# Row-sum reciprocals transposed in the tails' step, weighted sums one step later, one bank for each engine

## The chip, the cores and the metric

One core of a Trainium2 chip runs the whole program. The metric is the time of one execution on the device, in microseconds; a measurement is the median of several runs. TensorE (PE) multiplies matrices into PSUM, VectorE (DVE) and ScalarE (ACT) read PSUM and compute, GpSimd (POOL) works from SBUF alone, and SyncE (SP) issues the transfers. Each engine takes its instructions in the order in which the program puts them, and waits at an instruction for the semaphores that it names.

## The reference

An attention layer with a positional bias from a small network feeds a mixture of eight experts (one for each token), and that a gated feed-forward layer:

```python
scores = scale * np.matmul(q, k.transpose(0, 1, 3, 2))      # 4 batches, 8 heads, 576 x 576, head size 64
scores = scores + bias.transpose(2, 0, 1)[None, :, :, :]
scores = scores - np.max(scores, axis=-1, keepdims=True)
attn = np.exp(scores)
attn = attn / (np.sum(attn, axis=-1, keepdims=True) + 1e-09)
attn_out = np.matmul(attn, v)
...
h = np.maximum(x[mask] @ w1[e], 0.0)
out[mask] = gate_w[mask, None] * eom[mask, e, None] * (h @ w2[e])
...
return (silu * val @ w_out)
```

The change lies in the attention: the exponentials are multiplied by v before they are divided, and the division by the row sums is done on the product.

## The kernel before

The program computes the bias tables first, then the attention, then the experts, then the feed-forward layer. The attention is a loop over 16 **units**, a pair of heads p and a batch b each, and every unit has five **steps** c = 0 to 4 (c0 to c4 below). In c0 to c3 a step takes 128 queries of both heads, in c4 the last 64 queries of both heads at once, the one head on partitions 0 to 63 and the other on 64 to 127.

One pass of the loop over (unit, step) writes down, in this order, what goes into the engines' queues, and this hand-written order is what the chip follows (`tc.manual_schedule()`):

- **S** (s_pe, L255): PE multiplies queries and keys into a tile of two banks. There are two such tiles (pool pS, bufs=2); c0 to c3 need both, c4 needs one.
- **T** (t_pe, L288, L304, L305): PE transposes the exponentials of the step before the last one (`old`) into the tile T of two banks. 64x128 pieces on partitions 0 to 63 go to bank 0, those on 64 to 127 to bank 1. At c4 the `old` step is c2, and the tails (block 4) of c0 and c1 are transposed too, into **Tx**, the second of the pS tiles. At c1 `old` is c4 of the unit before.
- ACT's share of emptying T (t_ev with act=1, L309), into the tiles pt0 and pt1.
- **pv** (pv_list, L364): the matmuls of transposed exponentials by v, for the first 256 queries (list A, tile pv0) and the other 320 (list B, tile pv1). PVA and PVB say how many of a list's five go into which step.
- **s_max** (L259, DVE) adds the bias and finds the row's limit; **exp** (L264, ACT) makes the exponentials and the row sums.
- DVE's share of emptying T and Tx (t_ev with act=0, L311).
- **rps** (bc_recip, L347, L349, L352), in c1 and c3: the reciprocals of the sums, spread out along rows in the tiles rw and rt by POOL (p_recip), are transposed by PE into the free one of the pv banks and copied by ACT into the tile rb.
- p_recip (c0): DVE adds 1e-9 and takes reciprocals; POOL writes rw (L338) and rt (L340).
- **e0** (in c2 of the next unit) and **e1** (in c0 of the unit after that): DVE multiplies a finished pv tile by rb into xT (L370).
- one of the four pieces of the next unit's preparation on POOL: k_hi, k_lo, q_hi, q_lo (prep_qk).

DVE and ACT share T by columns: DVE takes the pieces 0 to 3 of both banks, ACT 4 to 7. In the last two units the router of the first batch runs in the loop's gaps (moe_early, at the places LG); behind the loop the last two `old` steps, the rest of the pv list (pvq) and the first expert steps (h_step, y_step) are written one by one.

Of the kernel before, what the change touches and what calls it, by code (L numbers as in the profile page):

```python
# [30 lines left out]
PVA = {4: 1, 5: 2, 6: 2}  # L31
PVB = {7: 2, 8: 2, 9: 1}
BL = (20, 28, 30, 32, 36)
VL = (7, 12, 13, 14)
LG = (1, 5, 5, 7, 8, 10, 10)
# [74 lines left out]
def body(tc, qt, kt, va, vb, ws, moe_w_gate, moe_w_output_gate, moe_w1, moe_w2, w_gate, w_val, w_out, ctab, cst, cst2, out):  # L110
    nc = tc.nc
    with ExitStack() as ctx:
# [27 lines left out]
        blocks, ident2 = const.tile([128, 128], F32, name="blocks"), const.tile([128, 64], F32, name="ident2")  # L140
# [149 lines left out]
        def t_pe(c, Es, x):  # L290

            t, E = tb["t"], Es[-1]
            if c == 2:
                for i in range(2):
                    t_blk(Es[i], x, 64 * i, 4)
            if c < 4:
                for j, n in enumerate((0, 1, 2, 3, 5, 6, 7, 8)):
                    t_blk(E, t, 64 * j, n)
            else:
# [4 lines left out]
                nc.tensor.transpose(t[0:64, 0, 384:448], E[0:64, 512:576], ident[0:64, 0:64])  # L304
                nc.tensor.matmul(t[64:128, 0, 384:448], E[64:128, 0:64], ident[64:128, 64:128], start=True, stop=True)  # L305
# [7 lines left out]
        def t_ev(p, b, c, x, act):  # L313

            t, pt = tb["t"], pts[p, b]
            if c < 4:
                o, n = 128 * (c % 2), 4 * act
                copy(act, pt[c // 2][:, n:n + 4, o:o + 128].rearrange("p n (r t) -> p r n t", r=2),
                     t[:, :, 64 * n:64 * n + 256].rearrange("p r (n t) -> p r n t", n=4))
                if c == 2 and not act:  # L320
                    copy(0, pt[0][:, 8].rearrange("p (c r t) -> p r c t", c=2, r=2), x[:, :, 0:128].rearrange("p r (c t) -> p r c t", c=2))
            elif act:
                copy(1, pt[1][:, 8, 0:256].rearrange("p (c r t) -> p r c t", c=2, r=2), t[:, :, 256:384].rearrange("p r (c t) -> p r c t", c=2))
                copy(1, pt[1][:, 8, 256:320], t[:, 0, 384:448])
# [6 lines left out]
        def p_recip(st):  # L331
# [3 lines left out]
            def f():  # L335
# [3 lines left out]
                rbs["t"] = ap.tile([128, S], F32, tag="E", bufs=4, name="rt")[:, 0:128]  # L339
                nc.gpsimd.tensor_scalar(rbs["t"], blocks, st[:, 38:39], None, ALU.mult)  # L340
            late.append(f)

        def bc_recip(p, b, st, f):

            ps, w = pv_tile(1 - f, "rps"), (256, 320)[f]
            for c in range(2):
                nc.tensor.transpose(ps[:, 128 * c:128 * c + 128], rbs["w"][:, 256 * f + 128 * c:256 * f + 128 * c + 128], ident)  # L347
            if f:
                nc.tensor.matmul(ps[:, 256:320], rbs["t"], ident2, start=True, stop=True)  # L349
            else:  # L350
# [436 lines left out]
        def consts():  # L787
            nc.gpsimd.memset(blocks, 0.0)
            for r in range(2):
                k = slice(64 * r, 64 * r + 64)  # L790
                nc.gpsimd.memset(blocks[k, k], 1.0)
# [531 lines left out]
```

## Time and profile before

| what | us |
|---|---|
| median of 3 runs | 1038.69 (1036.95 to 1039.5) |
| the profiled execution | 1042.37 |
| its span on the core | 1040.5 |
| PE busy | 995.6 (96%) |
| DVE busy | 574.5 (55%) |
| ACT busy | 439.7 (42%) |
| POOL busy | 123.9 (12%) |

The profile is of one execution. Busy shares are means over the whole program; the attention stage (about 85 to 320 us) has a balance of its own, which the stretches show. In a timeline an engine's instructions of one form that follow each other stand in one row: start, time, engine, line, operation, output and input tiles, count, and in brackets how long the engine was idle before it and what ended that. The end of a matmul is modelled, so that rows overlap by some tenths; the start of the next row tells better how long PE was with one. A float32 matmul that isn't a transpose makes two records.

### The profile page before, as it was taken

To read this page: it belongs to the slowest core of one execution; us is meant where nothing else is said; L and a number is where in the kernel's file an instruction comes from. 1 tells how busy PE (TensorE), PEld (TensorE's weight loads), DVE (VectorE), ACT (ScalarE), POOL (GpSimd) and SP (SyncE) were. 2 spreads that over 40 slices of the span, in tenths; PEclk is the share of its full clock that TensorE was granted. 3 is DMA by queue.
4 is the path that set the end of the run, shared out by engine and by line. 5 is a ranking of instruction groups with operands and counts; after the bars stand their busy time and mean duration, and the time that the engine had idled before them with its cause. 6 is when DMAs were issued, how large, how long until landed. Compare 5 with 4: busy or idle time off the path is not lost. (4 is left out here: it accounts for less than half of the span.)

```text
span 1040.5 us, 18771 instructions
## 1 busy us (share of the span) xinstructions
PE 995.6 (96%) x7477; PEld 802.3 (77%) x7477; DVE 574.5 (55%) x1257; ACT 439.7 (42%) x931; POOL 123.9 (12%) x122
## 2 busy tenths in 40 slices
PE   7978999999999999999999899999999999999998
PEld 2346767677667899998999677778888888888897
DVE  8966777677776654445565599952223223222322
ACT  6766766676665442332434445531113112211221
POOL 3662442433220000000000000000000000000000
PEclk9988999999999999999999999999999999999999
DMA  6774223342004052814733655511002000200010
GB/s 189 209 250 140 94 93 109 109 126 96 24 22 155 1 198 68 293 64 143 253 108 142 211 172 172 166 53 48 1 0 82 1 1 1 61 1 1 18 24 21
DMA packets 67754, 101.89 MB, mean 98 GB/s; under 512 B 9136, under 2 KB 37936, under 8 KB 67664
## 3 DMA queue, kind: packets, MB, share of 16 engines
q1 hardware_dynamic: 67504, 100.41, 30.5%
q8 instruction: 59, 0.97, 0.4%
q14 instruction: 31, 0.25, 0.1%
q10 hardware_dynamic: 160, 0.26, 0.1%
HBM read 74.63 MB, written 26.03 MB: 97 GB/s over the span
## 5 line engine op out<-in xcount | busy, mean ns | idle before, releaser
L1218 PE MATMUL v<-x,w 128*128 128x512 f32 (+1 forms) x720 | 161.5, 372 | 3.8 <-DVE w L967 3.8
L1218 PE MATMUL g<-x,w 128*128 128x512 f32 (+1 forms) x720 | 159.8, 371 | 2.1 <-DVE xl L722 2.0
L1218 PEld LDWEIGHTS v<-x,w 128*128 128x128 f32 x720 | 125.4, 189 | 32.1 <-DVE w L967 7.5
L1218 PEld LDWEIGHTS g<-x,w 128*128 128x128 f32 x720 | 127.4, 189 | 27.0 <-ACT x L1173 2.2
L1240 PE MATMUL o<-w,uh 128*128 128x512 f32 x432 | 133.4, 390 | 0.0
L1221 DVE TENSOR_TENSOR t<-g,t 128x512 f32<-128x512 f32 (+1 forms) x60 | 38.2, 636 | 169.6 <-ACT t L1220 169.6
L259 DVE CUSTOM_DVE_ANT_0 E<-S,bias 128x576 f32<-128x576 f32 x128 | 91.9, 755 | 47.4 <-PE S L255 24.3
L264 ACT ACTIVATE E<-E,st 128x576 f32<-128x576 f32 x144 | 110.0, 768 | 4.7 <-DVE st L259 4.7
L1220 ACT ACTIVATE t<-g 128x512 f32<-128x512 f32 (+1 forms) x60 | 33.2, 554 | 155.2 <-PE g L1218 155.2
L1225 ACT ACTIVATE uh<-t 128x512 fp32r<-128x512 f32 (+1 forms) x60 | 35.4, 589 | 146.0 <-DVE t L1222 146.0
L364 PE MATMUL pv<-pt,rawv 128*64 128x256 f32 (+1 forms) x640 | 95.5, 419 | 0.0
L255 PE MATMUL S<-kh,qz 64*128 64x288 f32 (+1 forms) x576 | 85.3, 328 | 10.5 <-DVE pt L311 6.4
L1240 PEld LDWEIGHTS o<-w,uh 128*128 128x128 f32 x432 | 80.3, 188 | 16.1
L255 PEld LDWEIGHTS S<-kh,qz 64*128 64x128 f32 (+1 forms) x576 | 58.7, 191 | 36.5 <-issue 22.7
L1240 PE MATMUL o<-w,ul 128*128 128x512 f32 x216 | 84.0, 389 | 0.0
L309 ACT ACTIVATE pt<-T 128x512 f32<-128x512 f32 (+1 forms) x96 | 46.2, 499 | 76.4 <-PE T L288 64.5
L573 ACT ACTIVATE qz<-T 128x288 fp32r<-128x288 f32 x63 | 25.8, 410 | 104.9 <-PE T L571 104.7
L574 DVE SCALAR_TENSOR_TENSOR qz<-T,qz 128x288 fp32r<-128x288 f32 x63 | 28.7, 456 | 72.9 <-ACT qz L573 72.5
L1222 DVE TENSOR_TENSOR t<-v,t 128x512 f32<-128x512 f32 (+1 forms) x60 | 38.3, 638 | 54.8 <-PE v L1218 53.5
L311 DVE COPY pt<-T 128x512 f32<-128x512 f32 x80 | 54.9, 687 | 7.7 <-ACT pt L309 7.7
L571 PE MATMUL T<-xh,whl 128*128 128x288 f32 x256 | 57.5, 300 | 1.4 <-ACT whl L532 0.7
L584 PE MATMUL y<-qz,whl 128*128 128x288 f32 x384 | 56.8, 296 | 1.3 <-DVE qz L574 0.9
(251 smaller groups left out, 1687.8 us busy)
## 6 DMA issues: line engine op xcount, KB each, us to landing
raww<-in_moe_w_dram SPq DMA_DIRECT2D x16, 768.0 KB, 6.1
bscr<-ob SPq DMA_DIRECT2D x36, 288.0 KB, 3.7
bias<-bscr SPq DMA_DIRECT2D x16, 576.0 KB, 4.3
rw<-in_w_gate_dram SPq DMA_DIRECT2D x12, 512.0 KB, 3.7
rw<-in_w_val_dram SPq DMA_DIRECT2D x12, 512.0 KB, 3.6
rw<-in_w_out_dram SPq DMA_DIRECT2D x12, 512.0 KB, 3.7
rawq<-in_qt_dram SPq DMA_DIRECT2D x16, 320.0 KB, 3.3
rawk<-in_kt_dram SPq DMA_DIRECT2D x16, 288.0 KB, 3.0
```

The source lines that it names most:

```text
L255: nc.tensor.matmul(t[:, f, 0:288], x[k, a], y[k, o], start=i == 0, stop=i == 2)
L259: nc.vector.tensor_tensor_reduce(out=E.rearrange("p (a b) -> p a b", a=2), in0=ps[:, :, 0:288], in1=bt[p, hh, c].rearrange("p (a b) -> p a ...
L264: nc.scalar.activation(E, E, AF.Exp, bias=st[:, 2 * c + hh:2 * c + hh + 1], scale=-1.0, accum_out=st[:, 10 + 2 * c + hh:11 + 2 * c + hh])
L309: nc.scalar.activation(o, x, AF.Copy)
L311: nc.vector.tensor_copy(o, x)
L364: nc.tensor.matmul(st["ps"][64 * hh:64 * hh + 64, 0:w], vt[p][:, hh, b, c, :], pts[p, b][f][:, c + 4 * hh if c < 4 else 8, :], start=c == ...
L571: nc.tensor.matmul(ps, wa[:, x, k], xs[k][y][:, o], start=k == 0 and i == 0, stop=k == 3 and i == 2)
L584: nc.tensor.matmul(hbuf["y"][d // 2][:, d % 2, 0:288], wb[:, x, d], t[:, y:y + 288], start=f == 0 and i == 0, stop=(one or f == 7) and i == 2)
L1218: nc.tensor.matmul(t, a[:, 128 * k:128 * k + 128], x, start=k == 0 and n == 0, stop=k == 3 and n == 2)
L1221: nc.vector.tensor_tensor(t, ps[0], t, ALU.mult)
L1222: nc.vector.tensor_tensor(t, ps[1], t, ALU.mult)
L1240: nc.tensor.matmul(ops[j][m], u[:, o], w, start=f == 0 and n == 0, stop=f == NF - 1 and n == 2)
```

## The change

- The reciprocals are not transposed apart from the rest (bc_recip goes). In c4, behind Tx's four pieces, ten transposes of 64x128 (r_blk) put the reciprocals of the unit before into the same tile Tx, beside the tails: eight from rw, two from the column of st that holds those of c4's rows. The tiles rt, blocks and ident2, and POOL's instructions for them, go.
- Tx is 448 columns of each bank, emptied into a new tile rb of two banks' width (rbs["n"]): ACT takes bank 1, DVE bank 0, and both take Tx ahead of T. T is shared by banks in the same way.
- p_recip moves from c0 to c1. The pv lists start one step later (PVA 5 to 7, PVB 8 to 10), and list A begins with the tails, read from rb. e0 moves from c2 to c4; e1 stays in c0, and is three instructions now: the 256 columns that both heads share, and 64 columns for each half of the partitions.
- For c4's rows POOL copies the first 64 columns behind the last (L925 of the changed kernel), so that two ordinary transposes take the place of the instructions of L304 and L305.
- The router's first piece moves by two places in LG, from c0 to c1. Behind the loop the order is written anew.

```diff
-PVA = {4: 1, 5: 2, 6: 2}
-PVB = {7: 2, 8: 2, 9: 1}
+PVA = {5: 1, 6: 2, 7: 2}
+PVB = {8: 2, 9: 2, 10: 1}
...
-LG = (1, 5, 5, 7, 8, 10, 10)
+LG = (3, 5, 5, 7, 8, 10, 10)
...
             if c == 2:
                 for i in range(2):
                     t_blk(Es[i], x, 64 * i, 4)
+                if st is not None:
+                    r_blk(st, [x[:, r, 128:448] for r in range(2)])
...
-                nc.tensor.transpose(t[0:64, 0, 384:448], E[0:64, 512:576], ident[0:64, 0:64])
-                nc.tensor.matmul(t[64:128, 0, 384:448], E[64:128, 0:64], ident[64:128, 64:128], start=True, stop=True)
+                t_blk(E, t, 384, 4)
...
-                o, n = 128 * (c % 2), 4 * act
-                copy(act, pt[c // 2][:, n:n + 4, o:o + 128].rearrange("p n (r t) -> p r n t", r=2),
-                     t[:, :, 64 * n:64 * n + 256].rearrange("p r (n t) -> p r n t", n=4))
-                if c == 2 and not act:
-                    copy(0, pt[0][:, 8].rearrange("p (c r t) -> p r c t", c=2, r=2), x[:, :, 0:128].rearrange("p r (c t) -> p r c t", c=2))
+                if c == 2:
+                    copy(act, rbs["n"][:, act, 0:w], x[:, act, 0:w])
+                o = 128 * (c % 2) + 64 * act
+                copy(act, pt[c // 2][:, 0:8, o:o + 64], t[:, act].rearrange("p (n t) -> p n t", n=8))
...
-        def bc_recip(p, b, st, f):
-
-            ps, w = pv_tile(1 - f, "rps"), (256, 320)[f]
-            for c in range(2):
-                nc.tensor.transpose(ps[:, 128 * c:128 * c + 128], rbs["w"][:, 256 * f + 128 * c:256 * f + 128 * c + 128], ident)
-            if f:
-                nc.tensor.matmul(ps[:, 256:320], rbs["t"], ident2, start=True, stop=True)
...
-            nc.scalar.activation(rbs[p, b][:, 256 * f:256 * f + w], ps[:, 0:w], AF.Copy)
+        def r_blk(st, t):
+
+            for c in range(5):
+                for r in range(2):
+                    k = slice(64 * r, 64 * r + 64)
+                    x = rbs["w"][k, 128 * c:128 * c + 128] if c < 4 else st[k, 38:39].to_broadcast([64, 128])
+                    nc.tensor.transpose(t[r][:, 64 * c:64 * c + 64], x, ident[k, k])
...
-                nc.vector.tensor_tensor(xT[p][:, b * S + o:b * S + o + w], st["ps"][:, 0:w], rbs[p, b][:, o:o + w], ALU.mult)
+                o, n, ps = b * S + 256 * f, rbs["n"], st["ps"]
+                nc.vector.tensor_tensor(xT[p][:, o:o + 256].rearrange("p (c r t) -> p c r t", c=2, r=2), ps[:, 0:256].rearrange("p (c r t) -> p c r t", c=2, r=2),
+                                        by_r(n[:, :, 128 + 128 * f:256 + 128 * f]), ALU.mult)
+                if f:
+                    for r in range(2):
+                        k = slice(64 * r, 64 * r + 64)
+                        nc.vector.tensor_tensor(xT[p][k, o + 256:o + 320], ps[k, 256:320], n[k, r, 384:448], ALU.mult)
...
-            if c in (1, 3) and ui:
-                bc_recip(*units[ui - 1], sts[ui - 1], c // 2)
-            if c == 0 and ui:
+            if c == 4:
+                nc.gpsimd.tensor_copy(E[:, 576:640], E[:, 0:64])
+            if c == 1 and ui:
                 p_recip(sts[ui - 1])
...
         t_pe(a[3], a[4], None)
-        t_ev(*a[1:4], None, 1)
-        t_ev(*a[1:4], None, 0)
+        t_ev(*a[1:4], None, 0, 1)
+        t_ev(*a[1:4], None, 0, 0)
...
-        pvs(2)
-        pvs(2)
+        pvs(2)
+        for f in ve[80]:
+            f()
+        pvs(4)
...
-        bc_recip(*units[15], sts[15], 0)
+        t = [t_tile() for _ in range(2)]
+        r_blk(sts[15], t)
+        n_tile()
+        for r in range(2):
+            copy(r, rbs["n"][:, r, 128:448], t[r][:, 0:320])
```

PE's queue of the kernel before at a c4 step, from the end of c3's pv to the start of c0 (rw and rt hold the spread reciprocals, E the exponentials):

```order
L364 MATMUL pv<-pt_2174,rawv 64x320 x4
L347 MATMUL rps<-ident,rw 128x128 [waits DVE_49]
L347 MATMUL rps<-ident,rw 128x128
L349 MATMUL rps<-ident_97,rt 128x64 [waits Pool_49]
L255 MATMUL S<-kh,qz_120 128x288 [waits DVE_49]
...
L288 MATMUL Tx<-ident,E 128x64 [waits DVE_49]
L288 MATMUL Tx<-ident,E 128x64 x3
L288 MATMUL T<-ident,E 128x64 [waits DVE_49]
L288 MATMUL T<-ident,E 128x64 x15
L364 MATMUL pv<-pt_2174,rawv 64x320 x2
L364 MATMUL pv<-pt_2412,rawv 64x256 [waits Activation_49]
```

The same place of PE's queue in the changed kernel:

```order
L369 MATMUL pv<-pt_2183,rawv 64x320 x4
L254 MATMUL S<-kh,qz_118 128x288 [waits DVE_49]
...
L287 MATMUL Tx<-ident,E 128x64 [waits DVE_49]
L287 MATMUL Tx<-ident,E 128x64 x3
L352 MATMUL Tx<-ident,rw 128x64 [waits Pool_49]
L352 MATMUL Tx<-ident,rw 128x64 x7
L352 MATMUL Tx<-ident,st 128x64 x2
L287 MATMUL T<-ident,E 128x64 [waits DVE_49]
L287 MATMUL T<-ident,E 128x64 x15
L369 MATMUL pv<-pt_2183,rawv 64x320 x4
```

The rps ahead of S is gone, ten transposes of the reciprocals stand between Tx's pieces and T, and the pv of the step are four of list B where they were two of each list.

DVE's queue of the kernel before, from s_max of c4 to s_max of c1 (an ISA row with E is an s_max, `st 128x1` reads its limit out):

```order
L259 ISA E,st<-S,biast 128x576 [waits PE_49]
L259 ISA st 128x1
L311 COPY pt_3366<-T 128x2x4x64 [waits Activation_49]
L311 COPY pt_3365<-Tx 128x2x2x64
L259 ISA E,st<-S,bias 128x576 [waits DVE_49,DMAHW0_49,PE_49,Pool_49]
...
L311 COPY pt_3366<-T 128x2x4x64 [waits Activation_49]
L333 TENSOR_SCALAR st<-st 128x9
L370 TENSOR_TENSOR xT_2651<-pv,rb 128x320
L336 RECIPROCAL st<-st 128x9 [waits DVE_49]
```

The same place of DVE's queue in the changed kernel:

```order
L258 ISA E,st<-S,biast 128x576 [waits PE_49]
L258 ISA st 128x1
L311 COPY rb<-Tx 128x448 [waits Activation_49]
L311 COPY pt_3395<-T 128x8x64 [waits Activation_49]
L374 TENSOR_TENSOR xT_2668<-pv,rb 128x256 [waits DVE_49]
L258 ISA E,st<-S,bias 128x576 [waits DMAHW0_49,PE_49]
...
L311 COPY pt_3395<-T 128x8x64 [waits Activation_49]
L374 TENSOR_TENSOR xT_2668<-pv,rb 128x256 [waits PE_49]
L379 TENSOR_TENSOR xT_2668<-pv,rb 64x64 x2
```

Tx's copy stands ahead of T's and waits for ACT now, e0 follows in c4, the copies of T go on waiting for ACT, and in c0 the sums' addition and reciprocal are gone and e1 has two small instructions more.

## Rows read from the trace of the kernel before

**Rows 1.** Stretches: length, busy us (instructions) of each engine, granted clock, DMA share, GB/s.
```profile
78.00:82.00 4.00, 2.66 (x24) 2.34 (x26) 2.34 (x6) 2.06 (x5) 0.00 (x0) 0.50 1.05 388
98.56:278.97 180.41, 175.71 (x2199) 126.53 (x2198) 130.75 (x337) 123.40 (x313) 66.86 (x76) 1.00 0.32 99
281.82:298.17 16.35, 14.34 (x172) 9.43 (x171) 10.58 (x31) 9.40 (x26) 4.91 (x6) 1.00 0.00 1
298.17:315.33 17.16, 16.18 (x201) 11.30 (x200) 14.09 (x50) 12.14 (x33) 1.19 (x2) 1.00 0.28 80
315.33:329.32 13.99, 12.66 (x126) 9.55 (x125) 9.55 (x21) 7.82 (x19) 2.01 (x3) 1.00 0.32 96
```
**Rows 2.** Timeline of PE, steps c4 and c0: start, us, what.
```profile
188.75 0.51 PE L255 MATMUL S<-kh,qz 128*128 128x288 f32 x2
...
189.71 0.34 PE L288 MATMUL Tx<-ident,E 64*128 64x64 f32 x4
189.88 0.66 PE L288 MATMUL T<-ident,E 64*128 64x64 f32 x16
...
191.59 0.40 PE L255 MATMUL S<-kh,qz 64*128 64x288 f32 x1
192.38 0.50 PE L255 MATMUL S<-kh,qz 64*128 64x288 f32 x3 [0.40 <-DVE pt L311]
...
193.16 0.75 PE L288 MATMUL T<-ident,E 64*128 64x64 f32 x16
```
**Rows 3.** Timeline of PE, steps c1, c2, c3 and the next c4.
```profile
194.85 0.63 PE L255 MATMUL S<-kh,qz 64*128 64x288 f32 x4
...
195.75 0.56 PE L288 MATMUL T<-ident,E 64*128 64x64 f32 x11
...
196.30 0.33 PE L305 MATMUL T<-ident,E 64*64 64x64 f32 x2
196.56 1.08 PE L364 MATMUL pv<-pt,rawv 128*64 128x256 f32 x8
197.57 0.44 PE L347 MATMUL rps<-ident,rw 128*128 128x128 f32 x2
197.94 0.53 PE L255 MATMUL S<-kh,qz 64*128 64x288 f32 x4
...
198.84 0.65 PE L288 MATMUL T<-ident,E 64*128 64x64 f32 x16
199.42 1.30 PE L364 MATMUL pv<-pt,rawv 128*64 128x320 f32 x8
200.65 0.53 PE L255 MATMUL S<-kh,qz 64*128 64x288 f32 x4
...
203.78 0.51 PE L255 MATMUL S<-kh,qz 128*128 128x288 f32 x2
```
**Rows 4.** Timeline of DVE: s_max of c3, then c4 from 203.78, e1 of c0.
```profile
201.75 0.76 DVE L259 CUSTOM_DVE_ANT_0 E<-S,bias 128x576 f32<-128x576 f32 x1 [0.34 <-PE S L255]
...
203.11 0.09 DVE L259 DVE_READ_ACCUMULATOR2_ANT st<- 128x1 f32 x1
...
205.06 0.76 DVE L259 CUSTOM_DVE_ANT_0 E<-S,biast 128x576 f32<-128x576 f32 x1 [1.27 <-PE Tx L288]
...
206.25 0.69 DVE L311 COPY pt<-T 128x512 f32<-128x512 f32 x1 [0.42 <-ACT pt L309]
...
206.86 0.42 DVE L311 COPY pt<-Tx 128x256 f32<-128x256 f32 x1
...
210.53 0.48 DVE L370 TENSOR_TENSOR xT<-pv,rb 128x320 f32<-128x320 f32 x1
```
**Rows 5.** Timeline of ACT: a copy of T in c4, and the rps copy behind the loop.
```profile
205.62 0.60 ACT L309 ACTIVATE pt<-T 128x512 f32<-128x512 f32 x1 [0.94 <-PE T L288]
...
325.18 0.36 ACT L352 ACTIVATE rb<-rps 128x256 f32<-128x256 f32 x1
```
**Rows 6.** Timeline of POOL: q_lo, the last piece of a unit's preparation.
```profile
214.53 1.56 POOL L223 TENSOR_TENSOR qz<-rawq,qz 128x640 fp32r<-128x640 f32 x1
```

More of the change, by code (lines that the diff above doesn't have):

```diff
@@ L358, in pv_list @@
             w = (256, 320)[f]
-            for c in range(5):
+            order = (0, 1, 2, 3, 4) if f else (4, 0, 1, 2, 3)
+            for c in order:
                 def m(c=c):
-                    if c == 0:
+                    if c == order[0]:
                         st["ps"] = pv_tile(f, "pv")
                     for hh in range(2):
-                        nc.tensor.matmul(st["ps"][64 * hh:64 * hh + 64, 0:w], vt[p][:, hh, b, c, :],
-                                         pts[p, b][f][:, c + 4 * hh if c < 4 else 8, :], start=c == 0, stop=c == 4)
+                        y = by_r(rbs["n"][:, :, 0:128]) if c == 4 and f == 0 else pts[p, b][f][:, c + 4 * hh if c < 4 else 8, :]
+                        nc.tensor.matmul(st["ps"][64 * hh:64 * hh + 64, 0:w], vt[p][:, hh, b, c, :], y, start=c == order[0], stop=c == order[4])
                 res.append(m)
             def ev():
-                o = 256 * f
-                nc.vector.tensor_tensor(xT[p][:, b * S + o:b * S + o + w], st["ps"][:, 0:w], rbs[p, b][:, o:o + w], ALU.mult)
+                o, n, ps = b * S + 256 * f, rbs["n"], st["ps"]
[3 more added lines that the diff above has]
+                    for r in range(2):
+                        k = slice(64 * r, 64 * r + 64)
+                        nc.vector.tensor_tensor(xT[p][k, o + 256:o + 320], ps[k, 256:320], n[k, r, 384:448], ALU.mult)
             return res, ev
@@ L787, in consts @@
         def consts():
[L788 to L791, printed above, removed]
-                nc.gpsimd.tensor_copy(ident2[k], ident[k, k])
             nc.sync.dma_start(cst_sb, cst)
@@ L902, in body @@
                 x = pS.tile([128, 2, 512], F32, tag="S", name="Tx") if c == 4 else None
-                t_pe(old[3], old[4], x)
-                t_ev(*old[1:4], x, 1)
+                w = 448 if ui else 128
+                if c == 4:
+                    n_tile()
+                t_pe(old[3], old[4], x, sts[ui - 1] if ui else None)
+                t_ev(*old[1:4], x, w, 1)
             E = ap.tile([128, 2 * S], F32, tag="ph", bufs=EB, name="E")
@@ L992, in body @@
         pvq = [f for n in sorted(pe) for f in pe[n]]
-        pvq = pvq[0:4] + [ve[82][0]] + pvq[4:7] + [both(pvq[7], lambda: bc_recip(*units[15], sts[15], 1))] + pvq[8:] + [ve[85][0]]
+        pvq = pvq[0:6] + [ve[84][0]] + pvq[6:] + [ve[85][0]]
         def pvs(n):
@@ L1056, in y_done @@
                 nc.sync.dma_start(x2[:, :, b].rearrange("d p n -> p d n"), hbuf["out"])
-        for f in ve[80]:
-            f()
         a, z = prev
         t_pe(a[3], a[4], None)
-        t_ev(*a[1:4], None, 1)
-        t_ev(*a[1:4], None, 0)
+        t_ev(*a[1:4], None, 0, 1)
+        t_ev(*a[1:4], None, 0, 0)
         p_recip(sts[15])
@@ L1076, in body @@
         m_conv(0, 1)
-        bc_recip(*units[15], sts[15], 0)
+        t = [t_tile() for _ in range(2)]
+        r_blk(sts[15], t)
+        n_tile()
+        for r in range(2):
+            copy(r, rbs["n"][:, r, 128:448], t[r][:, 0:320])
         for n in range(16 * B):
```

25 lines of the change are left out of this document (13 added, 12 removed).

## Prediction

> **What bounds it now.** First the stretches [rows 1]: twelve identical units of the attention stage take 180.41 us, 15.03 each, and PE is busy for 97% of them at a granted clock of 1.00. DVE has 10.9 of each 15 us, ACT 10.3 (130.75 and 123.40 over 12). So time is made by PE, and an engine matters only where PE stands still for it. Then PE's timeline through one unit [rows 2, 3]: five steps c4, c0, c1, c2, c3, each S, T (in c4 Tx before it), pv, sometimes rps. Read as start to next start:
>
> c4: S 0.96, Tx 0.17, T and pv 1.71: 2.84 us. c0: 3.26, where S takes 1.57 in place of the 0.90 of the other steps [rows 2]. c1: S 0.90, T 0.81, pv 1.01, rps 0.37: 3.09. c2: S 0.90, T 0.58, pv 1.23: 2.71. c3: the same and rps, 3.13, so this rps takes 0.42 [rows 3]. The sum is 15.03.
>
> The S of c0 is long because its second matmul waits for a DVE copy (the row says 0.40 idle; against an S without a wait 0.67 are lost). DVE's timeline of a c4 step shows why [rows 4]: s_max starts 1.28 us after S, the copy of T waits 0.42 us for ACT's copy, and Tx, whose buffer that S needs, is emptied last, ending 3.50 us after the step's start (207.28 against 203.78). PE could have begun S at 2.84.
>
> A second limit lies just under PE's. S has two buffers; the next step's S needs both s_max done. From S to the first s_max 1.10 us, from there to the end of the second 1.45 (201.75 to 203.20) [rows 3, 4]. A step of c0 to c2 can't be shorter than about 2.55 us, plus some 0.05 for the hand-over, however little PE has to do.
>
> After the attention stage PE is busy too; I take what the stage gains to arrive whole at the end, since weights there are loaded in an order that moves with the steps.
>
> **The change, part by part.** PE: both rps go, 0.37 + 0.42 = 0.79 a unit. In c1 the odd instructions of L304 and L305, which make T 0.81 long [rows 3], become two ordinary transposes; 16 such take 0.58 to 0.59, 0.037 each, so 14 take 0.51: 0.30 less. Added are ten transposes of 64x128 in c4, after Tx. I take 0.037 each, 0.37, since T's rows have the same shape on the same two halves of the array; the lower end of this is 0.037, the upper the 0.185 of rps's 128x128 transposes (two in 0.37) [rows 3], 1.85 us a unit. pv is as much work as before, one step later: c4 four pv of 320 columns (1.23), c0 half and half (1.13, today's c4), c1 and c2 the 256 ones (1.01), c3 1.23.
>
> Tx: ACT empties one bank (448 columns), DVE the other, and now before T. ACT: 0.36 for 256 columns and 0.60 for 512 [rows 5], 0.55 taken. DVE: 0.42 for 256 and 0.69 for 512 [rows 4], 0.62 taken. The order shows DVE's copies still waiting for ACT's, so splitting by bank frees neither of the other; I credit nothing for it.
>
> DVE: e1 becomes three instructions. Today 0.48 for 320 columns [rows 4]; 0.42 for the 256 of them, two of 64 columns between 0.07 (their columns alone) and 0.42 each. I take 0.15 to 0.2, nearest to the columns, so e1 costs about 0.7 to 0.8. It is the last thing in c0, and behind it stands s_max of c1. The sums' addition and reciprocal leave c0 for c1.
>
> ACT loses two copies of rps a unit (0.36 and somewhat more) and gains Tx (0.55) and one 64-column copy: even. POOL loses rt; rw moves behind k_lo; a copy of 64 columns is added in c4, and k_hi, k_lo, rw, q_hi and q_lo are queued behind it. The last, q_lo, ends today at 216.09 [rows 6], 0.4 us after c3 of its unit began (200.65 + 15.03 = 215.68); its reader is the S of the following c0, 5.5 us on, which covers the delay, and the reader of rw is c4, three steps behind the reciprocal. SP's issues keep their places.
>
> Walk through one new unit, c4's S at 0. c4: 0.96 + 0.17 + 0.37 + 0.58 + 1.23 = 3.31. The ten end at 1.50; ACT copies Tx from about 1.7 to 2.25, DVE (s_max ended at 2.05) from 2.3 to 2.92: Tx is free before 3.31, and c0's stall is gone. Behind DVE's waiting copy stand its T copy (to 3.5), e0 (to 3.9) and the s_max of c0, which isn't due before 4.41. c0: 0.90 + 1.69 + 0.12 (the half pv of 320) = 2.71, so 6.02; s_max runs 4.41 to 5.86, which fits. Then DVE: T copy, e1, free at about 7.1, just when c1's s_max wants to start (6.02 + 1.10 = 7.12). c1: PE 0.90 + 0.51 + 1.01 = 2.42, to 8.44, but s_max ends at 8.57 and its hand-over follows: 8.64. c2: 2.49, to 11.13, s_max ends at 11.19: 11.17. c3: 2.71, 13.88. **The unit falls from 15.03 to 13.88, by 1.15**: PE's own work falls by 1.39 (0.79 + 0.30 + 0.67 - 0.37), and 0.24 of it goes to the s_max chain, which is late next.
>
> The sum over the stage: 12 units by 1.15, 13.8. Before them unit 1's first four steps, where the pipeline starts a step later: 2.0. In the stretch of unit 14 with the router (16.35 us [rows 1]) the first PE wait for e1 goes but the waits for T's copies stay: 1.5, less 0.46 for the longer c4 ahead of it. In the next (17.16) DVE has the gates' work in c4 and c0 is released by it, so 0.55 is left. Behind the loop (13.99) two pairs of pv come on top (1.13), c4 is 0.46 longer, and the second h step now waits for ACT's copy out of the buffer it takes, which stands where 325.18 stands [rows 5] and is 0.4 to 0.5 longer; 0.8 of rps goes: a loss of 1.3. In all 2.0 + 13.8 - 0.46 + 1.5 + 0.55 - 1.3 = 16.1.
>
> **The profiled execution took 1042.37 us (span 1040.5), so 1026.3 after.** The runs' median, 1038.69, lies 3.7 lower: 1022.6, rounded 1022.7.
>
> **Rivals.** (a) The stall stays. If ACT's exps hold up its Tx copy, DVE's comes later still (it waits for ACT, as its T copy does for 0.42 today [rows 4]), and S of c0 waits as now. For it: two engines in a row where there was one. Against it: ACT is free 0.90 into c4 today (205.62 less 0.94 of idle time [rows 5], against 203.78), and Tx has 0.4 us to spare. Price: up to 0.67 by 13, 9 us: 1031.
>
> (b) Slower. The ten new transposes read a row-wide rw and, for two of them, a single column repeated; if each costs the 0.185 of an rps transpose, c4 is 4.79 long, the unit 15.36, and the stage loses 0.33 by 12; with the ends as above, in place of 16.1 less 1.48 by 14 = -4.6: 1043. It decides from 0.037 + 0.115 = 0.15 us a transpose. Against it: 16 in 0.58 today.
>
> (c) The clock. In [rows 1] the stretch at 0.50 (1.2 GHz, the lower level) lies at the stage's start, where PE is busy for 2.66 of 4 us; in the twelve units T, Tx and rps are over a quarter of PE's time and the granted clock is 1.00 (2.4 GHz). If c4's 30 transposes in a row brought it to the lower level, Tx, the ten and T would take 2.24 in place of 1.12, all the gain of the unit: some 1038. The Trainium skill, "TensorE: Matmul & The Clock Gate", Part 4: PE-mode transpose, says that transposes don't count as PE being busy, which would favour this case; the rows show over a quarter of the time in transposes without a fall, so the trace doesn't bear it out here. Also the clock's rise at the start may come a step later, since pv leaves the fifth step: 1 to 2 us, once.
>
> (d) The change does less than it says: only the rps go, the s_max chain takes the rest (all steps 2.75 or more): 0.7 a unit, 1028. This is inside the range.
>
> **Numbers.** Forecast 0.80, its own range 1017.5 to 1029 (the gain of a unit between 0.75 and 1.35, the ends by 2); (a) 0.11; (b) 0.04; (c) 0.03; 0.02 for what I don't see. (d) is part of the forecast's 0.80. The range of 8 in 10 reaches a little into (a): 1017 to 1032. A measurement of this kernel can tell about 0.3%, 3 us, from no change. Faster by more: forecast and (a), 0.91. Same: (c) and part of the unseen, 0.04. Slower: (b) and the rest, 0.05.
>
> **What would show it.** In the profile after: S of c0 at 0.90 with no wait for a DVE copy; the transposes of rw within 0.4 us; c1's T at 0.5; units of 13.7 to 14.3 us; PE's remaining idle time in front of S, released by s_max, in c1 and c2. I am wrong if Tx's copy ends later than c0's S could start, if rw's transposes are spaced by more than 0.1 us, if ACT's or POOL's rw copy releases Tx, or if the stage after gives the gain back in waits for weights.

## The result, and the profile after

The changed kernel takes 1022.41 us (median of 4 runs, 1021.46 to 1024.22) against 1039.10 for the kernel before beside it (1036.95 to 1041.48): a ratio of 0.984, 95% interval 0.9815 to 0.9867. Forecast was 1022.7, with a range of 1017 to 1032. The profiled execution of the changed kernel took 1021.46 us, its span 1019.3.

The stretches of the changed kernel that answer to [rows 1], cut at the same places of the program but for the end of the last (length, busy us and instructions of PE, PE's weight load, DVE, ACT and POOL, granted clock, DMA share, GB/s):

```profile
96.40:263.54 167.14, 166.85 (x2235) 120.54 (x2233) 138.04 (x361) 126.13 (x313) 62.52 (x76) 1.00 0.36 110
266.82:281.25 14.43, 12.41 (x166) 8.37 (x164) 10.12 (x32) 8.95 (x24) 5.21 (x7) 1.00 0.01 2
281.25:298.19 16.94, 15.22 (x203) 10.73 (x201) 14.49 (x51) 12.37 (x33) 0.97 (x2) 1.00 0.26 78
298.19:313.71 15.52, 13.91 (x150) 10.58 (x149) 11.51 (x25) 8.63 (x22) 1.30 (x3) 1.00 0.29 88
```

The twelve units take 167.14 us in place of 180.41, 13.93 each in place of 15.03, and they start 2.16 us earlier (96.40 against 98.56). The stretch with the router is 1.92 shorter and the one behind it 0.22. The last stretch of [rows 1] ends at 329.32, where the weights of the third h step are loaded; the step's first matmul starts at 329.45, and 313.71 in the changed kernel is that matmul. From matmul to matmul the end is 15.52 us long against 14.12, 1.40 longer. With 0.43 for the longer c4 ahead of the router (3.28, from 263.54 to 266.82, against 2.85) this is 2.16 + 13.27 - 0.43 + 1.92 + 0.22 - 1.40 = 15.74 us, which is what the third h step shows (329.45 before, 313.71 after). The medians differ by 16.7.

PE's timeline through one unit after, which answers to [rows 2, 3] (start, us, engine, line, operation, tiles, count, and in brackets the idle time before it):

```profile
193.91 0.53 PE L254 MATMUL S<-kh,qz 128*128 128x288 f32 x2
...
194.89 0.34 PE L287 MATMUL Tx<-ident,E 64*128 64x64 f32 x4
195.06 0.41 PE L352 MATMUL Tx<-ident,rw 64*128 64x64 f32 x8
195.31 0.22 PE L352 MATMUL Tx<-ident,st 64*128 64x64 f32 x2
195.37 0.66 PE L287 MATMUL T<-ident,E 64*128 64x64 f32 x16
...
197.19 0.53 PE L254 MATMUL S<-kh,qz 64*128 64x288 f32 x4
...
199.79 0.53 PE L254 MATMUL S<-kh,qz 64*128 64x288 f32 x4
...
200.69 0.59 PE L287 MATMUL T<-ident,E 64*128 64x64 f32 x14
...
202.23 0.92 PE L254 MATMUL S<-kh,qz 64*128 64x288 f32 x4
...
203.42 0.74 PE L287 MATMUL T<-ident,E 64*128 64x64 f32 x16
...
205.10 0.54 PE L254 MATMUL S<-kh,qz 64*128 64x288 f32 x4
```

The ten new transposes go from 195.06 to 195.37: 0.31 us. The S of c0 (197.19) runs through, four matmuls in one row with no wait, where [rows 2] show one matmul, 0.40 us of idle time and three more. c1's T has 14 transposes and takes 0.52, from 200.69 to the next pv at 201.21. What is new stands at 202.23: the first four matmuls of c2's S take 0.92 in place of 0.53. That S lasts 1.19 until T starts at 203.42, where those of c0, c1 and c3 last 0.90. The steps, start to start: c4 3.28, c0 2.60, c1 2.44, c2 2.87, c3 2.72.

DVE's timeline of the same c4, c0 and c1, which answers to [rows 4], with ACT's copy of Tx behind it:

```profile
195.21 0.76 DVE L258 CUSTOM_DVE_ANT_0 E<-S,biast 128x576 f32<-128x576 f32 x1 [0.76 <-PE Tx L287]
...
196.15 0.62 DVE L311 COPY rb<-Tx 128x448 f32<-128x448 f32 x1 [0.18 <-ACT rb L309]
196.70 0.69 DVE L311 COPY pt<-T 128x512 f32<-128x512 f32 x1
...
198.28 0.76 DVE L258 CUSTOM_DVE_ANT_0 E<-S,bias 128x576 f32<-128x576 f32 x1 [0.56 <-PE S L254]
...
200.25 0.41 DVE L374 TENSOR_TENSOR xT<-pv,rb 128x256 f32<-128x256 f32 x1
200.58 0.45 DVE L379 TENSOR_TENSOR xT<-pv,rb 64x64 f32<-64x64 f32 x2
201.05 0.76 DVE L258 CUSTOM_DVE_ANT_0 E<-S,bias 128x576 f32<-128x576 f32 x1
...
202.41 0.09 DVE L258 DVE_READ_ACCUMULATOR2_ANT st<- 128x1 f32 x1
```
```profile
195.57 0.55 ACT L309 ACTIVATE rb<-Tx 128x448 f32<-128x448 f32 x1 [0.67 <-PE Tx L352]
```

Tx is empty at 196.77, 2.86 us after c4's S, and c0's S comes at 3.28. e1 (200.25 to 201.03) is the last thing that DVE does before c1's s_max, which follows without a gap, 1.26 after c1's S. In fact DVE works without a gap from c0's s_max (198.28) to the end of c1's. That end is 202.50. S of c2 began at 202.23 in the one tile; its matmuls for the second head, in the other tile, start at 202.65.

### The profile page after: what moved, and what is told of

The parts are those of the page before. It is cut to its first block, busy times and chain, and to the rows that moved or that the text cites. A ratio compares the mean times of both kernels' runs of the same rounds, so it can differ in the third digit from the quotient of the medians.

```text
span 1019.3 us, 18850 instructions
## 1 busy us (share of the span) xinstructions
PE 976.4 (96%) x7525; PEld 790.2 (78%) x7525; DVE 584.0 (57%) x1290; ACT 443.6 (44%) x932; POOL 114.8 (11%) x117
## 5 line engine op out<-in xcount | busy, mean ns | idle before, releaser
L254 PE MATMUL S<-kh,qz 64*128 64x288 f32 (+1 forms) x576 | 82.8, 325 | 7.5 <-DVE st L258 6.7
L254 PEld LDWEIGHTS S<-kh,qz 64*128 64x128 f32 (+1 forms) x576 | 55.9, 188 | 43.1 <-DVE st L258 30.5
L369 PE MATMUL pv<-pt,rawv 128*64 128x320 f32 (+1 forms) x576 | 88.1, 422 | 0.0
L309 ACT ACTIVATE pt<-T 128x512 f32<-128x512 f32 (+2 forms) x112 | 49.6, 457 | 45.0 <-PE T L287 44.7
L1237 DVE TENSOR_TENSOR ul<-t,uh 128x512 fp32r<-128x512 f32 (+1 forms) x60 | 38.3, 638 | 32.3 <-ACT uh L1236 32.3
```

Source lines behind the costliest of these rows:

```text
L254: nc.tensor.matmul(t[:, f, 0:288], x[k, a], y[k, o], start=i == 0, stop=i == 2)
L309: nc.scalar.activation(o, x, AF.Copy)
L1237: pend.append(lambda: nc.vector.tensor_tensor(ul, t, uh.bitcast(F32), ALU.subtract))
```

## The experiments

Each run has its own comparison with the kernel before on the same chip. Of each I read the time first and then the length of the twelve units that answer to those of [rows 1].

### Undoing the stall alone, and bringing it back

The first kernel is the kernel before with Tx's copy ahead of T's in DVE's queue:

```diff
             if c < 4:
                 o, n = 128 * (c % 2), 4 * act
+                if c == 2 and not act:
+                    copy(0, pt[0][:, 8]..., x[:, :, 0:128]...)
                 copy(act, pt[c // 2][:, n:n + 4, o:o + 128]..., t[:, :, 64 * n:64 * n + 256]...)
-                if c == 2 and not act:
-                    copy(0, pt[0][:, 8]..., x[:, :, 0:128]...)
```

> The kernel before with one edit: in c4 DVE empties Tx ahead of T, where it emptied it behind T. Theory (the stall of c0's S is made by the place of Tx's copy in DVE's queue, and is 0.67 us of PE's time in each unit): DVE can copy Tx in the 0.42 us in which it waited for ACT's copy, Tx is free 2.5 us after c4's S in place of 3.5, c0's S takes 0.90 in place of 1.57, a unit of the twelve takes 14.36 in place of 15.03, and the time falls by 14 to 15 times 0.67, about 10 us, to 1029. Rival (the stall is only the first of two waits, and the s_max chain or a copy of T takes its place in c0 and c1): the unit stays above 14.8 and the time above 1036.

Measured: 1029.0 us (1026.84 to 1029.94) against 1039.53, ratio 0.9899 (0.9883 to 0.9916). The stretch of twelve units, a c4 and c0 on DVE, and the S of that c0 and the next c1 on PE:

```profile
95.73:268.06 172.33, 172.33 (x2200) 125.29 (x2198) 130.84 (x337) 123.37 (x313) 66.91 (x76) 1.00 0.33 104
```
```profile
198.19 0.42 DVE L311 COPY pt<-Tx 128x256 f32<-128x256 f32 x1
198.69 0.69 DVE L311 COPY pt<-T 128x512 f32<-128x512 f32 x1
...
200.95 0.75 DVE L259 CUSTOM_DVE_ANT_0 E<-S,bias 128x576 f32<-128x576 f32 x1
```
```profile
199.07 0.53 PE L255 MATMUL S<-kh,qz 64*128 64x288 f32 x4
...
201.57 0.72 PE L255 MATMUL S<-kh,qz 64*128 64x288 f32 x4
```

The copy of Tx takes the time in which DVE waited for ACT, the copy of T follows at once, and the stall is gone: PE shows no idle time in 172.33 us. A unit takes 172.33 / 12 = 14.36, 0.67 less than before. In the steps c0 gives 0.76 (2.50 in place of 3.26: its S 0.67, and its T, which no longer waits for the copy of the T before it, 0.10), and c1 takes 0.09 back: its S starts (201.57) before c0's second s_max has ended (201.70), and takes 0.97 until T. Two lines of code in another order, without the rest of the change, are worth 10 us, more than half of the change's gain.

The opposite: the changed kernel with both engines emptying Tx behind T.

```diff
-                if c == 2:
-                    copy(act, rbs["n"][:, act, 0:w], x[:, act, 0:w])
                 o = 128 * (c % 2) + 64 * act
                 copy(act, pt[c // 2][:, 0:8, o:o + 64], t[:, act]...)
+                if c == 2:
+                    copy(act, rbs["n"][:, act, 0:w], x[:, act, 0:w])
```

> The changed kernel with one edit: both engines empty Tx behind T in c4. Theory: ACT's Tx copy ends about 3.1 us after c4's S, DVE's, which waits for it, about 3.8 to 4.0, where c0's S is due at 3.29: c0's S is late by 0.5 to 0.7, the unit takes 14.4 to 14.6 in place of 13.93, and the time rises by 7 to 10 us to 1030 to 1032. Rival (with a bank for each engine the order doesn't matter, since the shorter c4 of before was what made the stall): the unit stays at 13.9 to 14.0 and the time within 1.5 us of 1022.4.

Measured: 1035.64 us (1033.18 to 1037.74), ratio 0.9957 (0.9942 to 0.9972): 13 us more than the changed kernel. The stretch, PE at a c0, and DVE at the c4 before it:

```profile
98.00:274.23 176.23, 170.40 (x2234) 122.69 (x2232) 138.78 (x361) 125.28 (x313) 62.37 (x76) 1.00 0.33 105
```
```profile
189.40 0.39 PE L254 MATMUL S<-kh,qz 64*128 64x288 f32 x1
190.28 0.50 PE L254 MATMUL S<-kh,qz 64*128 64x288 f32 x3 [0.49 <-DVE rb L311]
```
```profile
188.92 0.69 DVE L311 COPY pt<-T 128x512 f32<-128x512 f32 x1 [0.73 <-ACT pt L309]
189.52 0.61 DVE L311 COPY rb<-Tx 128x448 f32<-128x448 f32 x1
```

A unit takes 14.69, a little more than the 14.4 to 14.6 expected; the S of c0 takes 1.66. The same stall is back, and the order in which the copies stand is its cause. The time rose by more than the 7 to 10 us expected: 0.76 by 12 units are 9.1, and the rest of the 13 lies outside the units. In this execution they began 1.60 us later than in the one of the changed kernel (98.00 against 96.40), and its mean granted clock is 0.986 against 0.994, with lower stretches behind the attention. One of the six executions had a mean clock of 0.993, within the 0.991 to 0.994 of the changed kernel's four: it took 1033.18, 10.8 more than their median, which is 0.76 by 14. The others had lower clocks (0.984 to 0.991) and took longer; whether the edit brings that about isn't shown.

### The price of the ten transposes

The changed kernel with the ten written twice:

```diff
-                if st is not None:
+                for _ in range(0 if st is None else 2):
                     r_blk(st, [x[:, r, 128:448] for r in range(2)])
```

> The changed kernel with the ten transposes of the reciprocals written twice in every unit of the loop (the second ten write the same columns again). Theory (a transpose costs 0.031 us and nothing waits for their end): c4 grows from 3.29 to 3.60, the unit from 13.93 to 14.24, the time by 15 times 0.31, 4.6 us, to 1027. Rival (they cost more than their spacing, because Tx is emptied later and c0's S waits for it): c0's S takes more than 0.90, the unit 14.4 or more, the time 1030 or more. Rival on the other side (they stand beside a wait and cost nothing): the unit stays at 13.93.

Measured: 1025.31 us (1024.13 to 1026.93), ratio 0.9863 (0.9847 to 0.988). The twelve units, and PE in a c4:

```profile
95.48:266.37 170.89, 170.67 (x2354) 124.33 (x2353) 137.99 (x361) 126.08 (x313) 62.40 (x76) 1.00 0.34 108
```
```profile
196.33 0.41 PE L352 MATMUL Tx<-ident,rw 64*128 64x64 f32 x8
...
196.64 0.41 PE L352 MATMUL Tx<-ident,rw 64*128 64x64 f32 x8
...
196.95 0.66 PE L287 MATMUL T<-ident,E 64*128 64x64 f32 x16
```

The second ten go from 196.64 to 196.95, 0.31 us, as the first, and the unit takes 14.24, 0.31 more: 0.031 us a transpose, all of it on PE's path, and no more. The repeated column of st costs as little as rw (195.31 to 195.37 for two in the changed kernel). 15 times 0.31 is 4.6; the time rose by 2.9, within the intervals. With forty transposes in a row in each c4 the granted clock of the stretch stays at 1.00, so the prediction's case (c) has no support here either.

### A bank for each engine

The changed kernel with T shared by columns as before, Tx by banks:

```diff
-                o = 128 * (c % 2) + 64 * act
-                copy(act, pt[c // 2][:, 0:8, o:o + 64], t[:, act]...)
+                o, n = 128 * (c % 2), 4 * act
+                copy(act, pt[c // 2][:, n:n + 4, o:o + 128]..., t[:, :, 64 * n:64 * n + 256]...)
```

> The changed kernel with T shared as before, DVE the columns of pieces 0 to 3 of both banks and ACT those of 4 to 7; Tx stays one bank for each engine. Theory (a bank for each engine brings nothing by itself, since DVE's copy waits for ACT's either way): the unit stays at 13.93 within 0.05, the time within 1 us of 1022.4. Rival (the two engines hinder each other in one bank, so the split by banks is a part of the gain): DVE's or ACT's copies of T take longer by 0.1 or more each, the unit 14.1 or more, and the time 1025 or more.

Measured: 1022.2 us (1020.57 to 1023.42), ratio 0.9826 (0.9809 to 0.9842).

```profile
96.31:263.51 167.20, 166.92 (x2235) 120.57 (x2233) 138.03 (x361) 126.17 (x313) 62.45 (x76) 1.00 0.35 110
```

167.20 us against 167.14, the busy times of DVE and ACT the same to 0.04: this part of the change does nothing.

### What the s_max chain takes back

The three kernels of this part ran beside the changed kernel itself.

> The changed kernel as it is, beside the three that follow, so that they are compared on the same chip: 1022.4 within 1.5 us, a unit of 13.93.

It took 1022.48 us (1021.55 to 1025.37), ratio 0.9838 (0.982 to 0.9856), twelve units 167.20.

One part undone, the odd transposes of c4's second piece in c1:

```diff
-                t_blk(E, t, 384, 4)
+                nc.tensor.transpose(t[0:64, 0, 384:448], E[0:64, 512:576], ident[0:64, 0:64])
+                nc.tensor.matmul(t[64:128, 0, 384:448], E[64:128, 0:64], ident[64:128, 64:128], start=True, stop=True)
...
-                for r in range(2):
-                    k = slice(64 * r, 64 * r + 64)
-                    copy(1, pt[1][k, 8, 256:320], t[k, r, 384:448])
+                copy(1, pt[1][:, 8, 256:320], t[:, 0, 384:448])
...
-            if c == 4:
-                nc.gpsimd.tensor_copy(E[:, 576:640], E[:, 0:64])
```

> The changed kernel with one part undone: the two odd instructions that transposed c4's second piece in c1 are back, and POOL's copy of 64 columns in c4 and one of ACT's two small copies are gone again. Theory (in c1 and c2 the s_max chain and not PE sets the pace, so that what PE saves in c1 is waited for in front of c2's S): c1's T takes 0.81 in place of 0.52, c2's S 0.90 to 0.95 in place of 1.19, c1 and c2 together stay at 5.32 within 0.1, and the time within 1.5 us of 1022.4. Rival (PE's work counts in full): the unit grows by 0.30 to 14.23, the time by 15 times 0.30, to 1026.9.

Measured: 1023.16 us (1022.45 to 1025.82), ratio 0.9842 (0.9824 to 0.986).

```profile
96.34:264.69 168.35, 168.35 (x2247) 123.10 (x2245) 138.04 (x361) 122.64 (x301) 60.21 (x64) 1.00 0.35 110
```

The unit grows by 0.10 (168.35 against 167.20 over twelve): in its steps c1's T is back at 0.81 and c2's S falls from 1.19 to 1.01. The rival, with 0.30, falls. The theory fits better, but it had c2's S at 0.90 to 0.95 and no growth. Where the 0.10 comes from stands in c0, on DVE:

```profile
198.97 0.76 DVE L258 CUSTOM_DVE_ANT_0 E<-S,bias 128x576 f32<-128x576 f32 x1 [0.67 <-PE S L254]
```

This s_max starts 1.20 after the S of c0, where it is 1.10 in the changed kernel (means of the twelve units). From there on both kernels go alike: 2.77 us on, with DVE busy all the time, c1's s_max starts, and 2.37 after that c2's T. So PE's 0.29 in c1 costs nothing; it goes into the wait in front of c2's S. Why s_max starts later in c0 no run shows.

Then e1 split into its 256 columns (e1[0]) and the two pieces of 64 (e1[1]):

```diff
-                at_step(ve, 5 * ui + 10, e1)
+                at_step(ve, 5 * ui + 10, e1[0])
+                at_step(ve, 5 * ui + 11, e1[1])
...
-            if c == 1 and ui:
+            if c == 2 and ui:
                 p_recip(sts[ui - 1])
```

> The changed kernel with DVE's work in c0 and c1 moved: of e1's three instructions the two of 64 columns (0.45 us) stand a step later, in c1, and the reciprocals of the sums in c2 in place of c1. Theory (c1's s_max starts late because e1 ends late, 1.26 after c1's S where 1.10 would do): c1's s_max starts 0.16 earlier, c2's S falls from 1.19 to 1.05 within 0.05, the unit by 0.12 to 0.16, the time by 14 times that, 1.7 to 2.3 us, to 1020.4. Rival (s_max is released by S and not by e1, 0.2 after the matmuls' end): no change in the unit, 1022.4. Rival on the other side (what is moved into c1 and c2 makes the s_max of c2 or c3 late): c3's S takes over 0.95, the unit 13.9 or more.

Measured: 1021.78 us (1021.07 to 1023.26), ratio 0.9826 (0.981 to 0.9841). The stretch, and DVE from e1's 256 columns on:

```profile
95.60:261.60 166.00, 166.00 (x2234) 120.65 (x2233) 138.05 (x361) 126.11 (x313) 62.05 (x77) 1.00 0.36 112
```
```profile
198.79 0.41 DVE L374 TENSOR_TENSOR xT<-pv,rb 128x256 f32<-128x256 f32 x1
199.49 0.76 DVE L258 CUSTOM_DVE_ANT_0 E<-S,bias 128x576 f32<-128x576 f32 x1 [0.29 <-PE T L287]
```

The unit falls by 0.10, to 13.83, c2's S to 1.09. Now DVE is idle for 0.29 us before c1's s_max, so e1 no longer holds it, and still 0.19 of c2's S stays over 0.90. I had expected 0.12 to 0.16, taking 1.10 us from S to s_max; here it is 1.16 (198.33 to 199.49). So of the 0.29 that c2's S lost in the changed kernel, a third is DVE's queue; two thirds remain, and there S, s_max of two heads and the hand-over take that time with two S tiles. The gain in time, 0.7 us, is too small for these runs.

### The order behind the loop

e1 split, and the code behind the loop in another order:

```diff
+        m_conv(0, 1)
+        t = pS.tile([128, 2, 512], F32, tag="S", name="rS")
+        r_blk(sts[15], [t[:, r] for r in range(2)])
+        n_tile()
+        for r in range(2):
+            copy(r, rbs["n"][:, r, 128:448], t[:, r, 0:320])
         h_step(mu[0]["ws"], mu[0]["xs"], 0, ps=...)
         pT.close()
...
-        m_conv(0, 1)
-        t = [t_tile() for _ in range(2)]
-        r_blk(sts[15], t)
-        n_tile()
-        for r in range(2):
-            copy(r, rbs["n"][:, r, 128:448], t[r][:, 0:320])
```

> The kernel before it (e1 split) with the order behind the loop changed too: the last reciprocals are transposed into the second S tile ahead of the first h step, in place of the T tiles behind it, and the second weights are converted ahead of that h step. Theory (PE stands still for 1.41 us in front of the second h step because ACT's copy of the reciprocals, queued behind 1 us of conversions, has to empty the tile that it takes): the idle time goes, 1.2 to 1.5 us, and the time is 1018.9 within 1.5. Rival (the second h step then waits for its own weights, which are converted no earlier than 1 us behind the last T copy): under 0.5 us, 1020.

Measured: 1018.15 us (1017.6 to 1021.62), ratio 0.9798 (0.9779 to 0.9818) against 0.9838 for the changed kernel beside it: 4.3 us less than that, and the shortest time of all. In the changed kernel, PE ahead of the second h step, and ACT there:

```profile
309.53 0.40 PE L580 MATMUL T<-xh,w1hl 128*128 128x288 f32 x1 [1.41 <-ACT rb L309]
```
```profile
308.01 0.62 ACT L541 ACTIVATE w1hl<-raww 128x512 fp32r<-128x512 f32 x1
308.53 0.62 ACT L541 ACTIVATE w2hl<-raww 128x512 fp32r<-128x512 f32 x1
309.05 0.43 ACT L309 ACTIVATE rb<-T 128x320 f32<-128x320 f32 x1
```

In this kernel, PE at the end of the first h step, the start of the second and that of the third:

```profile
305.20 0.29 PE L582 MATMUL h<-xh,w1hl 128*128 128x288 f32 x1
305.34 0.30 PE L582 MATMUL T<-xh,w1hl 128*128 128x288 f32 x1
...
309.60 0.30 PE L582 MATMUL T<-xh,w1hl 128*128 128x288 f32 x1
```

The 1.41 us are gone. From the last unit's c4 (295.73) to the third h step it takes 13.87 us, against 15.52 in the changed kernel and 14.12 in the kernel before: 1.65 less than in the changed kernel. With 1.2 from the twelve units this explains some 3 of the 4.3 us; for the rest the profiles show no place, and it is within the width of the intervals.

### Two more readings

The kernel before without bc_recip:

```diff
-            if c in (1, 3) and ui:
-                bc_recip(*units[ui - 1], sts[ui - 1], c // 2)
...
-                nc.vector.tensor_tensor(xT[p][...], st["ps"][:, 0:w], rbs[p, b][:, o:o + w], ALU.mult)
+                nc.vector.tensor_tensor(xT[p][...], st["ps"][:, 0:w], ones[:, o:o + w], ALU.mult)
```

> The kernel before without the transposes of the reciprocals and their copies (bc_recip): e0 and e1 multiply by a tile of ones, so the weighted sums are not divided by the row sums, and the routing of the experts behind the attention may differ; only the units of the attention are read. Theory (the rps stand on PE's path with their whole time): c1 falls from 3.09 to 2.72 and c3 from 3.13 to 2.71, c0 keeps its stall (3.26), the unit falls from 15.03 to 14.24. Rival (the s_max chain takes a part back, as in the changed kernel): c2's or c1's S takes more than 0.95 and the unit stays above 14.35.

```profile
98.78:271.02 172.24, 167.52 (x2126) 120.36 (x2124) 130.80 (x337) 116.41 (x289) 66.99 (x76) 1.00 0.34 106
```

A unit takes 14.35, 0.68 less than before, of 0.79 expected: c1 2.72 and c3 2.71 as the theory says, c0 keeps its 3.25, and 0.08 goes to c2, whose T takes 0.66 in place of 0.58, and 0.03 to c4. The unit lies on the rival's bound, but not where the rival has it: the S of c1, c2 and c3 take no more than 0.91. (The one execution took 1027.9 us; since what follows the attention may differ, that isn't compared.) So the rps stood on PE's path with nearly all of their time.

And a try for more, on top of the kernel with the shortest time: one pv of list B out of c4.

```diff
-PVB = {8: 2, 9: 2, 10: 1}
+PVB = {8: 2, 9: 1, 10: 1, 11: 1}
...
-                at_step(ve, 5 * ui + 10, e1[0])
+                at_step(ve, 5 * ui + 11, e1[0])
```

> The kernel with e1 split and the new order behind the loop, and one pv pair of list B moved on: list B has one in c4 (two before), one in c0 and the last in c1, and all of e1 in c1. Theory (c4 is bound by PE alone at 3.29, and c1 has PE standing still for about 0.2 us, so 0.31 of work taken from c4 is put where 0.2 of it is free): c4 2.98, c0 2.61, c1 2.75, c2 2.50, c3 2.72 to 2.87, the unit 13.56 to 13.71 in place of 13.83, the time 1.7 to 3.5 us less, 1015.5 within 1.5. Rival (a shorter c4 brings back the stall of c0's S, since Tx is free only 2.9 after c4's S): c0's S over 1.0 and the unit at 13.8 or more, 1018.5.

Measured: 1021.67 us (1019.23 to 1024.32), ratio 0.9819 (0.9794 to 0.9843).

```profile
97.20:263.00 165.80, 165.80 (x2234) 121.61 (x2233) 138.13 (x361) 126.16 (x313) 61.92 (x77) 1.00 0.36 112
```

The units take 165.80 us against 165.97 with the pv where it was, which is nothing. I mis-sized what moved: a pv pair of list B is 0.54, not 0.31. c4 falls to 2.75 and c2 to 2.50, but c0 grows to 2.78 (S 0.95 and T 0.70, since Tx and T are emptied no earlier for that), c1 to 2.97 and c3 to 2.81. What one step saves, the others pay. The median is 3.5 us above that without this edit, but the two were measured on different chips, and the intervals of their ratios overlap (0.9794 to 0.9843 and 0.9779 to 0.9818): that the edit costs time isn't shown, only that it brings none of the expected gain. In the profiles the stretch of the last unit is 0.34 longer (17.48 against 17.14) and the end behind it 0.52 (14.39 against 13.87).

## Why the prediction was right, point by point

| term, us | predicted | measured |
|---|---|---|
| rps gone, a unit | 0.79 | 0.68 when taken out alone |
| c1's odd instructions, a unit | 0.30 | 0.29 less work; put back, the unit grows by 0.10 |
| stall of c0's S, a unit | 0.67 | 0.67 when taken away alone |
| ten transposes, a unit | 0.37 | 0.31 |
| taken back by the s_max chain, a unit | 0.24 | 0.39 |
| gain of a unit | 1.15 | 1.11 |
| before the twelve units | 2.0 | 2.16 |
| c4 ahead of the router | -0.46 | -0.43 |
| stretch with the router | 1.5 | 1.92 |
| the next stretch | 0.55 | 0.22 |
| behind the loop | -1.3 | -1.40 |
| sum | 16.1 | 15.7 to the third h step, 16.7 in the medians |

**The bound** was read rightly: the unit's time is PE's work and PE's waits. The 166.85 of 167.14 us in which PE is busy don't show this by themselves, since a matmul that is held counts as busy: in c2's S the second head starts 0.42 after the first and no idle time is listed. (The prediction, too, books the stall of 0.67 as PE's own work, where it is a wait.) The two terms that carry the sum, the rps and the stall, were each shown by an edit of its own; put together with the price of the transposes and the 0.10 of the odd instructions, what they brought or cost when changed alone (0.68 + 0.67 + 0.10 - 0.31 = 1.14) comes near the 1.11 of the whole. What a single edit brings is already net of waits, so the table's 0.39 isn't to be taken off that sum again. The other parts of the change, the pv lists a step later and e0 in c4, were not tried alone.

**The stall** went for the reason given. Tx's copy ends 2.86 us after c4's S (2.92 forecast) and the order of the copies alone brings the stall back. Case (a) of the prediction fell, since ACT's copy starts 1.66 after c4's S and takes 0.55, as forecast. Case (d), with all steps at 2.75 or more, fell too: c0, c1 and c3 take less.

**The ten transposes** cost 0.031 each, and the choice of the near row (0.037, [rows 2, 3]) against the far one (0.185) was right; case (b) needed 0.15. Case (c) fell as well: the granted clock of the twelve units is 1.00 with 30 transposes in a row in each c4, and with 40. The Trainium skill, "TensorE: Matmul & The Clock Gate", Part 4: PE-mode transpose, says that a transpose doesn't count as PE being busy in the same way as other matmuls. The trace shows no effect of that for transposes with matmuls on either side.

**What was mis-sized** is what the s_max chain takes back. The walk through the unit put 2.62 and 2.53 on c1 and c2, 5.15 together; they take 5.32 (mean of the twelve units). e1 costs 0.78 as forecast, but c1's s_max starts 1.26 after its S rather than 1.10, and the hand-over to c2's S costs 0.15 (202.50 to 202.65) where 0.05 was taken. The 1.26 is mostly c0's doing: PE is done with c0 in 2.60 where the walk had 2.71, because T of c0 no longer waits, while DVE's queue runs on from c0's s_max as before. What PE gains in c0 it waits for in c2. From c0's S to the end of c2 it is 7.92 us against 7.86 in the walk, so the error of the chain itself is small. Both runs on this chain agree that it, and not PE, sets c1 and c2 together: PE's work put back into c1 leaves the way from c0's s_max to c2's T as long as it was, and DVE's work taken out of it gives back 0.10.

**Before the twelve units** the number was right, but its reason, the pipeline that starts a step later, isn't shown. From the c4 before them (82.53 in the kernel before) to their start it takes 16.03 us before and 13.80 after, 13.15 in the second profile of the changed kernel, 14.24 in the kernel before with only Tx's copy moved ahead, and 16.02 in the changed kernel with the copies behind. So the order of the copies, which moves no step, comes with 1.8 of it. In the kernel before, the S of the c0 between them waits as those of the twelve units do:

```profile
87.20 0.50 PE L255 MATMUL S<-kh,qz 64*128 64x288 f32 x3 [0.93 <-DVE pt L311]
```

The granted clock also rises from 0.50 to 1.00 at different points there, between 82 and 84 us in the second profile of the changed kernel and in that with the moved copy, after 84 in the others, and with the copies behind it is at 0.57 once more from 88 to 92. So how much of the 1.8 us is the wait and how much the clock stays open. The terms of the router's stretch and of the one behind it were not tried alone.

**Behind the loop** the second h step waits for ACT's copy as forecast: two conversions of weights stand ahead of that copy in ACT's queue, and PE stands still for 1.41 us. That isn't all new. The kernel before stood still at the same place too, for the first of these conversions:

```profile
324.81 0.40 PE L571 MATMUL T<-xh,w1hl 128*128 128x288 f32 x1 [0.85 <-ACT w1hl L532]
```

With 0.19 more inside its second h step this is 1.04, so the wait grew by 0.37; from the first h step to the pv behind the second it is 5.49 us against 5.16, 0.33 longer. The 0.4 to 0.5 of the forecast were about right. What it didn't see is that the whole wait can go, as the other order shows.

**The base.** The profiled execution of before and that of after differ by 20.9 us, not 16.1, and the forecast of 1026.3 for an execution like the one profiled is off by 4.8. The medians differ by 16.7, and the forecast from the median by 0.3. Of the 20.9 us 15.7 are there at the third h step; the other 5.2 come behind it, where the profile of before has two falls of the granted clock (last section) and that of the changed kernel none. I estimate these falls at some 3 us, their length times the part of the clock that is missing; the rest isn't explained. Taking the difference from the profile and the base from the median avoided this. That the forecast lands within 0.3 us is luck in part: the units gave 0.5 us less than forecast, the router's stretch 0.4 more, and the 1.0 us between 15.7 and the medians' 16.7 is within the width of the measurement (14 to 19 us by the interval of the ratio).

## What to carry to other kernels

When an engine that is at its bound waits for a buffer, look at which copy empties that buffer and what stands ahead of it in the copying engine's queue: two copies exchanged were worth 10 us here, more than the work that was saved beside them. Work saved on the bounding engine counts only down to the next chain, so name that chain's length (here S, two s_max and the hand-over, some 2.65 us a step over c1 and c2) before adding up savings. When work is moved behind a loop, look at what is queued ahead of the moved instruction: here another order of the same work took away a wait of 1.41 us.

## What the runs showed of the hardware

A float32 transpose of a 64x128 piece, in alternation on the two halves of the array, costs 0.031 to 0.037 us, with a column repeated 128 times as input too, and with forty in a row in each unit the granted clock stays at 1.00. On DVE two products of 64 partitions by 64 columns take 0.45 together, beside 0.41 for 128 by 256 and 0.62 for a copy of 448 columns: some 0.22 each, where the columns alone would have given about 0.1 (a quarter of the 0.41).

Executions of like code differ in two places that have nothing to do with the change. The twelve units of the same changed kernel began at 96.40 in one profile and at 94.65 in another. And at the end of the first batch of experts PE is idle for 1.34 or 1.35 us with little work after it, in every profile; in some executions the granted clock goes to 0.5 (1.2 GHz, the lower of the two levels) right behind it and in others it stays at 1.00. Stretches there of the changed kernel:

```profile
455.00:457.50 2.50, 1.78 (x15) 1.71 (x16) 1.17 (x10) 0.00 (x0) 0.13 (x1) 1.00 0.04 7
457.50:460.00 2.50, 2.50 (x21) 2.32 (x20) 0.73 (x3) 0.41 (x1) 0.00 (x0) 1.00 0.76 163
```

and of the kernel with T shared by columns, whose attention takes the same time:

```profile
455.00:457.50 2.50, 1.84 (x12) 1.77 (x13) 1.14 (x9) 0.00 (x0) 0.13 (x1) 0.80 0.06 11
457.50:460.00 2.50, 2.50 (x12) 2.50 (x12) 0.46 (x1) 0.41 (x1) 0.00 (x0) 0.52 0.79 190
```

In the second row PE does 12 matmuls in place of 21. The profiled execution of the kernel before had such a fall twice (0.51 from 475.0 to 477.5, and 0.66 from 582.5 to 587.5), that of the changed kernel not once. What decides which way an execution goes was not tried.
